# The first third of w_mod in four column transfers, applied in two parts, and 330 operations in a new order

## The chip, the cores and the metric

The kernel runs on one core of a Trainium2 chip. The metric is the device time of one execution in microseconds. Before the change it is 325.63 us, the median of 3 runs (325.49 to 326.61). The profile is of one further execution, whose span from the first to the last instruction is 324.3 us.

## The reference, cut to what matters

A transformer block with conditioning: six vectors of 640 numbers come from one product of `silu(c)` with `w_mod`, and shift, scale and gate an attention with a sliding window of 256 and a gated MLP.

```python
mod = (silu(c) @ w_mod).reshape(1, 6, 1, -1)          # c: 1 x 640, w_mod: 640 x 3840
sa, ca, ga, sb, cb, gb = mod[:, 0], ..., mod[:, 5]
h = layernorm(x) * (1 + ca) + sa                      # x: 2048 x 640
x = x + ga * attention(h @ wqkv, window 256, 32 heads of 20) @ wo
h = layernorm(x) * (1 + cb) + sb
x = x + gb * ((sigmoid(h @ w_gate) * (h @ w_up)) @ w_down)
```

The change concerns `sa` and `ca`, the first two of the six vectors: columns 0 to 1279 of `w_mod`, which is its first third.

## The kernel before

The 2048 rows of `x` are taken in eight chunks of 256 rows (two blocks of 128). A chunk goes through layernorm, modulation, q/k/v projection, scores, exponentials, masks, the product with V, output projection, second layernorm and MLP. Chunks overlap: the projections of later chunks are mixed into the attention and the MLP of earlier ones.

The program first writes down a list of 2121 operations (`Prog.op`, L91). Each gets a number from the list `PRIO` (L342), by its place in the list of operations. `schedule` (L152) sorts by that number; the number modulo 5 names the engine (0 TensorE, 1 ScalarE, 2 VectorE, 3 GpSimd, 4 SyncE). So `PRIO` fixes both the engine of an operation and its place in that engine's queue, and each queue is worked off strictly in that order. `schedule` also estimates times, but uses them only to choose which buffer of a pool a tile gets. `emit` (L250) adds the semaphore waits: an operation waits for all that it reads and for the last users of its buffer.

**The loads at the start.** SyncE issues block 0 of `x`, then the first third of `w_mod` in five transfers of 128 rows each (`load_bulk` at L624, target `wd`; 2560 contiguous bytes per row), then `wqkv` in pieces of 320 columns for q and k (`load_w3`, L615, called at L626; 640 bytes per row and piece) and one piece of 640 columns for v. Between these stand further blocks of `x`. ScalarE issues `c` and block 1 of `x`.

**The modulation vectors.** TensorE first transposes `c` (L634); ScalarE and VectorE make `silu(c)` and spread it to 64 equal columns (`silubc`). `fnA` (L750) then multiplies each 128x128 tile of the loaded third with `silubc`: fifty matmuls of 64 columns, in five operations by rows (`kt`), each waiting for one transfer, all accumulating in one tile of PSUM, `psA`. Between them stand short filler matmuls on zeros (`fill`, L657, instructions at L660). One VectorE copy (L761) takes the result to `mA`, which holds shift and scale for the five column tiles of 128 (`dt` 0 to 4).

**Chunk 0.** VectorE normalizes blocks 0 and 1 (L796), TensorE transposes them, two small matmuls per `dt` (`pe_transposes`, L816; the one of `dt` 4 goes to a free bank of `psA`), ScalarE and VectorE copy the five results to `hT` (L839) and then modulate `hT` in place, ten operations of 128x128, one per `dt` and block (L846, L847). All ten read `mA`. Then the projections begin: for a block and a piece of 320 columns there are five matmuls over `kt` in two operations (`pe_chain`, L674), the first with `kt` 0 and 1, the second with `kt` 2 to 4. They wait for their piece of `wqkv` and for their parts of `hT`.

**Before the first transposes** TensorE runs ten matmuls on zeros (`warm`, L646, instructions at L649).

Of the kernel before, what the change touches and what calls it, by code (L numbers as in the profile page):

```python
# [13 lines left out]
D = 640  # L14
# [3 lines left out]
NDT = D // 128  # L18
# [7 lines left out]
SWITCH = 0.095  # L26
ENGATTR = {"pe": "tensor", "act": "scalar", "dve": "vector", "pool": "gpsimd", "sp": "sync"}
ENGS = ("pe", "act", "dve", "pool", "sp")
OVERLAP = {"pe": 0.0, "act": 0.085, "dve": 0.075, "pool": 0.045, "sp": 0.0}
# [52 lines left out]
class Prog:  # L82
# [69 lines left out]
    def schedule(self):  # L152


        free = {e: START for e in ENGS}
        bw = 0.0
        lastturn = False
        order = {e: [] for e in ENGS}
        dmacnt = [0] * NDMA
        dmalast = [None] * NDMA  # L160
        rr = 0
        pemode = 0
        portend = 0.0
        freed = {}

        def slot_time(pool, s):
            ten = pool.tenant[s]
            if ten is None:
                if not all(x.done for x in pool.init[s]):
                    return None  # L170
                return max([x.end + x.lat for x in pool.init[s]], default=0.0)
            return None if ten.left else freed[ten]

        def take(t, s):
            ten = t.pool.tenant[s]
            t.prev = list(t.pool.init[s]) if ten is None else list(ten.rel)
            t.slot = s
            t.pool.tenant[s] = t

        for o in sorted(self.ops, key=lambda x: x.prio):  # L180
            assert all(d.done for d in o.deps), o.tag
            e = ENGS[o.prio % 5]
            assert e in o.engs, (o.tag, e)
            o.eng = e
            st = max([o.tmin, free[e] + (SWITCH if e == "pe" and o.mode != pemode else 0.0)]
                     + [d.end + (0.0 if d.eng == "pe" and e == "pe" else d.lat) for d in o.deps])
            if o.isdma and e == "sp":
                st = max(st, bw - QMAX)
            for t in o.tiles:
                if t.slot is None:  # L190
                    step = 1 if t.mate is None else 2
                    best = None
                    for s in range(0, len(t.pool.tenant), step):
                        rts = [slot_time(t.pool, s + k) for k in range(step)]
                        if None not in rts and (best is None or max(rts) < best[0]):
                            best = (max(rts), s)
                    assert best is not None, (o.tag, t.name)
                    if t.mate is None:
                        take(t, best[1])
                    else:  # L200
                        take(t, best[1] + t.odd)
                        take(t.mate, best[1] + 1 - t.odd)
                for x in t.prev:
                    st = max(st, x.end + x.lat)
            if e == "dve" and o.port:
                st = max(st, free["pool"])
            elif e == "pool":
                st = max(st, portend)
            o.start = st
            if e == "pe":  # L210
                pemode = o.mout
            dur = o.dur[e]
            free[e] = st + dur - OVERLAP[e]
            if e == "dve" and o.port:
                portend = free[e]
            if o.isdma:
                turn = o.dlat > 3.0
                if e == "sp" and bw - st > 2.0:
                    free[e] += 0.35 if o.dur[e] > 1.0 else 0.1
                bw = max(st + o.dlat, bw + (MIXED if turn != lastturn and bw > st + o.dlat else 0.0)) + o.work  # L220
                lastturn = turn
                o.end = max(bw - 0.83, st + dur)
                s = rr
                rr = (rr + 1) % NDMA
                dmacnt[s] += 16
                o.key, o.val = f"d{s}", dmacnt[s]
                if dmalast[s] is not None:
                    o.deps.append(dmalast[s])
                dmalast[s] = o
            else:  # L230
                o.end = st + dur
            order[e].append(o)
            o.done = True
            for t in o.tiles:
                t.left -= 1
                if t.left == 0:
                    last = {}
                    for x in t.ops:
                        if x.isdma:
                            last[x] = x  # L240
                    for e2 in ENGS:
                        xs = [x for x in t.ops if x.eng == e2 and not x.isdma]
                        if xs:
                            last[e2] = max(xs, key=lambda x: x.start)
                    t.rel = list(last.values())
                    freed[t] = max(x.end + x.lat for x in t.rel)
        self.order = order
        self.span = max(o.end for o in self.ops)
# [88 lines left out]
def c_pe(n):  # L337
# [3 lines left out]
PE_EPS = 0.14  # L341
PRIO = [  # L342
# [132 lines left out]
MW = 64  # L475
# [831 lines left out]
```

## Time and profile before

| | us |
|---|---|
| median of 3 runs | 325.63 |
| lowest, highest | 325.49, 326.61 |
| span of the profiled execution | 324.3 |
| busy in it: TensorE | 317.3 |
| busy: VectorE, ScalarE, GpSimd | 211.8, 212.3, 187.2 |
| moved by DMA | 37.85 MB, 117 GB/s on average |

From 4 us to 20 us the DMA engines are kept busy: the windows of 4 us there show between 352 and 378 GB/s. TensorE's busy time counts each matmul to a modelled end, so that pipelined matmuls overlap; a busy share near 100% means that the queue did not run dry, and the step from one matmul's start to the next says how fast it went.

The lines of the profile stand with the prediction. In a timeline a row is: start, duration, engine, line of the kernel, operation, target<-sources with their shapes, count of instructions merged into the row, and in brackets the idle time before it with what ended it. PE is TensorE's matmul, PEld its weight load, which may run ahead of the matmul; DVE is VectorE, ACT ScalarE, POOL GpSimd, SP SyncE. A row of windows gives for a stretch its length, then for each engine the busy time and the number of instructions, the granted clock, the busy share of the DMA engines, and GB/s.

### The profile page before, as it was taken

The numbers are of one execution on the slowest core, as the hardware profiler recorded it, in microseconds if no ns is written. First come the engines' busy times: TensorE is split into PE (matmuls) and PEld (weight loads), VectorE is DVE, ScalarE is ACT, GpSimd is POOL, SyncE is SP. The second block draws the span as 40 slices with busy tenths as digits, with TensorE's granted clock in tenths as the row PEclk, the third lists the DMA queues.
The fourth block names the chain that finished last, engine by engine and source line by source line (L and its number), as shares of the span: only waits on it lengthen the run. The fifth ranks groups of instructions, "written<-read, shape, count | busy, mean of one in ns | idle before, by whom it ended". The sixth has DMA issues, their size and how long they took to land.

```text
span 324.3 us, 11594 instructions
## 1 busy us (share of the span) xinstructions
PE 317.3 (98%) x4872; PEld 222.7 (69%) x4873; DVE 211.8 (65%) x424; ACT 212.3 (65%) x316; POOL 187.2 (58%) x276
## 2 busy tenths in 40 slices
PE   8999999989999999999999999999999999999997
PEld 3564545446776568765776467877786788787885
DVE  5797898778687959674477475837463769264332
ACT  1899985889876687788687867786767764011120
POOL 5128869976668694847585939382939691012100
DMA  7998799989891383824405394340213032202101
GB/s 249 371 333 299 165 269 180 200 137 183 260 164 22 83 109 77 152 61 101 85 22 82 97 103 110 92 69 5 81 40 88 3 79 53 76 20 64 40 2 40
DMA packets 71694, 37.85 MB, mean 117 GB/s; under 512 B 45274, under 2 KB 70362, under 8 KB 71642
## 3 DMA queue, kind: packets, MB, share of 16 engines
q1 hardware_dynamic: 69616, 35.31, 48.3%
q10 hardware_dynamic: 2026, 1.80, 2.1%
q8 instruction: 38, 0.62, 0.8%
q14 instruction: 14, 0.11, 0.1%
HBM read 21.30 MB, written 5.25 MB: 82 GB/s over the span
## 4 chain that ended last, share of the span: by engine, by line
PE 73%; DMA 2%; SPq 2%; DVE 1%; POOL 1%; issue 0%; DVEq 0%
PE M L668 61%; PE S L669 6%; PE M L669 5%; DMA gbc<-gate 2%; SPq L803 2%; DVE wd L1192 1%; POOL x L793 0%; POOL st L788 0%; DVE hh L1211 0%; POOL E L1040 0%; DVE x L1230 0%; DVEq L310 0%
## 5 line engine op out<-in xcount | busy, mean ns | idle before, releaser
L1040 POOL TENSOR_SCALAR_AFFINE_SELECT E<-E 128x512 bf16<-128x512 bf16 (+1 forms) x176 | 142.6, 836 | 68.7 <-ACT E L1015 67.0
L1015 ACT ACTIVATE E<-S 128x512 bf16<-128x512 f32 (+2 forms) x184 | 150.9, 878 | 47.4 <-PE S L669 46.5
L668 PE MATMUL M<-wqkv,hT 128*128 128x480 bf16 (+1 forms) x340 | 73.9, 355 | 0.6 <-ACT hT L846 0.5
L668 PE MATMUL M<-h2T,wu 128*128 128x256 bf16 x480 | 68.0, 273 | 0.5 <-DVE hh L1211 0.5
L668 PE MATMUL M<-h2T,wg 128*128 128x256 bf16 x480 | 67.8, 273 | 0.0
L668 PE MATMUL M<-wd,hh 128*128 128x320 bf16 (+2 forms) x396 | 58.1, 295 | 0.0
L1209 ACT ACTIVATE sig<-M 128x512 f32<-128x512 f32 x48 | 28.9, 602 | 44.1 <-PE M L668 41.7
L1211 DVE SCALAR_TENSOR_TENSOR hh<-sig,M 128x512 bf16<-128x512 f32 x48 | 32.4, 681 | 37.1 <-ACT sig L1209 24.0
L668 PEld LDWEIGHTS M<-h2T,wu 128*128 128x128 bf16 x480 | 45.9, 98 | 8.4 <-issue 1.2
L668 PEld LDWEIGHTS M<-h2T,wg 128*128 128x128 bf16 x480 | 45.7, 98 | 7.1
L668 PEld LDWEIGHTS M<-wqkv,hT 128*128 128x128 bf16 x340 | 30.1, 98 | 27.6 <-DMA wqkv<-in_A_wqkv_dram 1.6
L668 PEld LDWEIGHTS M<-wd,hh 128*128 128x128 bf16 x396 | 36.8, 98 | 14.3 <-DVE hh L1211 0.2
L669 PEld LDWEIGHTS S<-QT,KT 20*64 20x64 bf16 (+1 forms) x1856 | 19.9, 100 | 21.3 <-ACT E L1015 12.0
L1230 DVE TENSOR_TENSOR x<-M,x 128x320 bf16<-128x320 f32 (+2 forms) x33 | 15.6, 476 | 27.2 <-PE M L668 27.2
L669 PE MATMUL S<-QT,KT 20*64 20x256 bf16 (+5 forms) x1856 | 32.1, 228 | 1.2 <-ACT E L1015 1.2
L776 DVE BATCH_NORM_STATS2 st<-x 128x6 f32<-128x320 bf16 x64 | 28.6, 477 | 2.3 <-DMA x<-in_A_x_dram 1.9
L1082 DVE STREAM_TRANSPOSE T<-M 128x512 f32<-128x512 f32 x32 | 21.5, 698 | 9.2 <-PE S L669 8.0
L668 PE MATMUL M<-wo,oT 128*128 128x320 bf16 x160 | 25.4, 299 | 0.0
L669 PE MATMUL M<-E,V 128*32 128x128 bf16 (+1 forms) x960 | 22.8, 246 | 0.8 <-ACT E L1015 0.4
L781 POOL TENSOR_SCALAR st<-st 128x2 f32<-128x2 f32 x16 | 3.7, 234 | 33.8 <-DVE st L778 33.6
L669 PEld LDWEIGHTS M<-E,V 128*32 128x32 bf16 x960 | 19.2, 97 | 5.3 <-issue 2.9
L1091 DVE STREAM_TRANSPOSE On<-Tn 128x1024 bf16<-128x1024 bf16 x16 | 19.8, 1240 | 0.3
(77 smaller groups left out, 240.2 us busy)
## 6 DMA issues: line engine op xcount, KB each, us to landing
x<-in_A_x_dram SPq DMA_DIRECT2D x23, 160.0 KB, 2.3
doc<-On SPq DMA_DIRECT2D x56, 40.0 KB
wd<-in_B_w_down_dram SPq DMA_DIRECT2D x4, 480.0 KB
wd<-in_w_mod_dram SPq DMA_DIRECT2D x5, 320.0 KB
wqkv<-in_A_wqkv_dram SPq DMA_DIRECT2D x4, 400.0 KB
wu<-in_w_mod_dram SPq DMA_DIRECT2D x5, 320.0 KB
oT<-doc SPq DMA_DIRECT2D x8, 192.0 KB, 2.5
out_dram<-x SPq DMA_DIRECT2D x9, 160.0 KB
```

What stands on the lines that cost most here:

```text
L668: return e.matmul(o, l, r, start=st, stop=sp, skip_group_check=True)
L669: return e.matmul(o, l, r, start=st, stop=sp, tile_position=tp, skip_group_check=True)
L776: A("dve", lambda e, g, bi=bi, j=j: e.bn_stats(v(bi * 12 + j * 6, 6), src[bi].ap[:, j * 320:(j + 1) * 320]), 0.48, reads=[src[bi].r()], wr ...
L781: A("pool", lambda e, g: e.tensor_scalar(v(28, n), var(), EPS, None, op0=ALU.add), 0.2, reads=[st.r(("m", bi)) for bi in range(n)], writes ...
L803: return e.dma_start_transpose(dst(), src())
L1015: A("act", lambda e, eng: e.activation(dst(), src(), ACT.Exp, scale=SM_SCALE), c_act(n), reads=[Sp.r()], writes=[E.r(key)], prio=3, tag=f" ...
L1040: A("pool", lambda e, eng: e.affine_select(rows(dst), rows(src), pattern=[[0, 8], [sign, n]], compare_op=ALU.is_ge, fill=0.0, base=base, c ...
L1082: A("dve", lambda e, g, h=h: e.transpose(T1.ap[:, 512 * h:512 * h + 512], X[h].ap), 0.694, reads=[X[h].r()], writes=[T1.r(h)], prio=3.5, t ...
L1091: A("dve", lambda e, g: e.transpose(On.ap[:], Tn.ap[:]), 1.22, reads=[Tn.r()], writes=[On.r()], prio=4, tag=f"tr2_{a}")
L1209: A("act", lambda e, g, pg=pg, sg=sg: e.activation(sg.ap[:], pg.ap[:], ACT.Tanh, scale=0.5), c_act(512), reads=[pg.r()], writes=[sg.r()], ...
L1211: A("dve", lambda e, g, pu=pu, sg=sg, f0=f0: e.scalar_tensor_tensor(out=hh.ap[:, f0:f0 + 2, :], in0=sg.ap[:].rearrange("p (a b) -> p a b", ...
L1230: A("dve", lambda e, g, ps=ps, bi=bi, c0=c0, n=n: e.tensor_tensor(x1[bi].ap[:, c0:c0 + n], ps.ap[:, 0:n], x1[bi].ap[:, c0:c0 + n], op=ALU. ...
```

## The change

1. The first third of `w_mod` comes in four transfers by columns: scale tiles 0 to 2, shift tiles 0 to 2, scale tiles 3 and 4, shift tiles 3 and 4. The first two are 128 x 5 pieces of 768 bytes, the last two of 512 bytes.
2. `fnA` becomes four operations, one per transfer, each over all five `kt`. They accumulate in two banks of `psA`, and two VectorE copies take the result to `mA`: tiles 0 to 2 after the second transfer, tiles 3 and 4 after the fourth. A modulation of chunk 0 reads only its own part. The matmul that opens the accumulation becomes two.
3. Of the fillers, two single ones stay; a third single one and a double one after the last `fnA` go.
4. Block 4 of `x` is issued behind `wqkv`'s v piece instead of ahead of the second q piece.
5. `PRIO` is new. The second part of every engine's queue keeps its order (the last 816 of TensorE's operations, 279 of ScalarE's, 338 of VectorE's, 224 of GpSimd's, 179 of SyncE's); ahead of it the order differs.
6. `schedule` no longer estimates times; the buffer of each tile stands in a new list `SLOTS`, which holds the same buffers that the estimate gave before.

```diff
-    load_bulk(wm_ap[0], wm_src[:, :, 0:1280], Rm[0], 0.93, 0.2, "wm0", lat=0.9)
+    CG = (range(0, 3), range(3, 5))
+    PIECES = [(G, bank) for G in range(2) for bank in (1, 0)]
+    R_wc = {x: R(f"wc{x[0]}{x[1]}") for x in PIECES}
+    for k, (G, bank) in enumerate(PIECES):
+        lo, hi = bank * D + CG[G][0] * 128, bank * D + CG[G][-1] * 128 + 128
+        dma(lambda lo=lo, hi=hi: wm_ap[0][:, :, lo:hi], lambda lo=lo, hi=hi: wm_src[:, :, lo:hi], 0.0036 * (hi - lo),
+            writes=[R_wc[G, bank]], prio=0.2 + 0.01 * k, tag="wm0", lat=0.9)
...
-    for kt in range(NDT):
-        def fnA(e, g, kt=kt):
-            for bank in (1, 0):
-                for cg in range(5):
-                    ins = mm(e, psA.ap[:, bank, cg * MW:cg * MW + MW],
-                             wm_ap[0][:, kt, bank * D + cg * 128:bank * D + cg * 128 + 128], silubc[:, kt, 0:MW],
-                             kt == 0 and cg == 0 and bank == 0, kt == NDT - 1)
+    for n, (G, bank) in enumerate(PIECES):
+        def fnA(e, g, G=G, bank=bank):
+            for kt in range(NDT):
+                for cg in CG[G]:
+                    j = (1 - bank) * len(CG[G]) + cg - CG[G][0]
+                    ins = mm(e, psA.ap[:, G, j * MW:j * MW + MW],
+                             wm_ap[0][:, kt, bank * D + cg * 128:bank * D + cg * 128 + 128], silubc[:, kt, 0:MW], False, kt == NDT - 1)
             return ins
-        if 0 < kt < 4:
+        if 0 < n < 3:
             fills.append(fill(FILL, oA[-1:]))
...
-    fills.append(fill(2 * FILL, oA[-1:]))
-    A("dve", lambda e, g: e.tensor_copy(mA[:], psA.ap[:, 0:2, 0:5 * MW].rearrange("p b (a m) -> p b a m", m=MW)[:, :, :, 0]), 0.18,
-      reads=[psA.r()], writes=[R_mA], prio=0)
+        if bank == 0:
+            lo, hi = CG[G][0], CG[G][-1] + 1
+            A("dve", lambda e, g, G=G, lo=lo, hi=hi: e.tensor_copy(
+                mA[:, :, lo:hi], psA.ap[:, G, 0:2 * (hi - lo) * MW].rearrange("p (b a m) -> p b a m", b=2, m=MW)[:, ::-1, :, 0]), 0.18,
+              reads=[psA.r((G, 1)), psA.r((G, 0))], writes=[R_mAg[G]], prio=0, tag="mAc")
...
-                    A(("act", "dve"), mo, {"act": 0.44, "dve": 0.28}, port=True, reads=[dst.r(("t", dt))] + Rmod, writes=[dst.r((dt, bi))],
+                    A(("act", "dve"), mo, {"act": 0.44, "dve": 0.28}, port=True, reads=[dst.r(("t", dt)), Rmod[dt > 2]], writes=[dst.r((dt, bi))],
```

The two lists `PRIO`, read as queues, begin as follows (q0 is the projection of block 0 with the first q piece, k0 the one with the first k piece; a and b are a chain's first operation, `kt` 0 and 1, and its second, `kt` 2 to 4; T is a transposition on TensorE of projected q or k).

| queue | before | after |
|---|---|---|
| SyncE | x0, five of w_mod, q piece 1, k piece 1, x3, x2, k piece 2, x4, q piece 2, v piece, x5 | x0, four of w_mod, q piece 1, k piece 1, x3, x2, k piece 2, q piece 2, v piece, x4, x5 |
| TensorE | fnA, fill, fnA, fill, fnA, fill, fnA, transposes of `dt` 1, 0, 2, 3, 4, last fnA, double fill, q0a, q0b, k0a, k0b, block 1 q a and b, T, T, block 1 k a, ... scores | fnA scale 0-2, fill, fnA shift 0-2, fill, fnA scale 3-4, transposes of `dt` 1, 4, 0, 2, 3, fnA shift 3-4, q0a, k0a, k0b, q0b, block 1 q a and b, block 1 k a, T, T, ... scores |
| VectorE | normalize x1, x0, copy to hT twice, copy to `mA`, modulate 6 times, statistics of x3 and x2, ... statistics of x4 | normalize x1, x0, first copy to `mA`, copy to hT once, modulate `dt` 1 and 0 of block 0, second copy to `mA`, modulate 6 times, statistics of x2 and x3, ... |
| ScalarE | copy to hT three times, modulate 4 times, take out q0, k0 | copy to hT four times, modulate twice, take out k0, q0 |

Up to the first score matmuls TensorE has the same projections and transpositions in both lists.

More of the change, by code (lines that the diff above doesn't have):

```diff
@@ L152, in schedule @@
     def schedule(self):
-        free = {e: START for e in ENGS}
-        bw = 0.0
-        lastturn = False
         order = {e: [] for e in ENGS}
@@ L161, in schedule, with number @@
         rr = 0
[L162 to L178, printed above, removed]
+        tiles = {}
+        def number(t):
+            if t is not None and t not in tiles:
+                tiles[t] = len(tiles)
+                number(t.mate)
+        for o in self.ops:
+            for t in o.tiles:
+                number(t)
         for o in sorted(self.ops, key=lambda x: x.prio):
@@ L184, in schedule @@
             o.eng = e
[L185 to L188, printed above, removed]
             for t in o.tiles:
                 if t.slot is None:
[L191 to L215, printed above, removed]
-            if o.isdma:
[L217 to L223, printed above, removed]
-                rr = (rr + 1) % NDMA
[L225 to L231, printed above, removed]
+                    s = SLOTS[tiles[t]] if SLOTS else 0
@@ new lines, in schedule @@
+                    ten = t.pool.tenant[s]
+                    assert ten is not None or all(x.done for x in t.pool.init[s]), (o.tag, t.name)
+                    assert ten is None or ten.left == 0, (o.tag, t.name)
+                    t.prev = list(t.pool.init[s]) if ten is None else list(ten.rel)
+                    t.slot = s
+                    t.pool.tenant[s] = t
+            if o.isdma:
+                dmacnt[rr] += 16
+                o.key, o.val = f"d{rr}", dmacnt[rr]
+                if dmalast[rr] is not None:
+                    o.deps.append(dmalast[rr])
+                dmalast[rr] = o
+                rr = (rr + 1) % NDMA
@@ L237, in schedule @@
                     last = {}
[L238 to L244, printed above, removed]
+                    for x in sorted(t.ops, key=lambda x: x.prio):
+                        last[x if x.isdma else x.eng] = x
                     t.rel = list(last.values())
-                    freed[t] = max(x.end + x.lat for x in t.rel)
         self.order = order
-        self.span = max(o.end for o in self.ops)
     def emit(self):
@@ L338, in c_pe @@
     return max(n, 64) / 2400.0 + 0.0027
-PE_EPS = 0.14
 PRIO = [
[117 rows of a table removed]
[116 rows of a table added]
+]
+SLOTS = [
[20 rows of a table added]
 ]
@@ L466 @@
 DSAFE = 1.5
-START = 0.8
-PORTLAG = 0.05
-MIXED = 0.55
 NPB = 0
@@ L484 @@
 WSE = (("dve", "pool"), ("dve", "pool"))
-QMAX = 4.5
 WDT = 72.0
@@ L743, in build, with ones @@
     A("pool", lambda e, g: e.memset(Eall[:, 1, 0:5 * MW], 1.0), 0.3, writes=[R_one], prio=0)
-    p_E.init[1].append(A("pe", lambda e, g: mm(e, psA.ap[:, 1, 0:5 * MW], ident[:], Eall[:, 1, 0:5 * MW], True, False), 0.14,
-                         reads=[R_one, R_ident], writes=[psA.r()], prio=0, lat=0.2, tag="modA"))
+    def ones(e, g):
+        for G in range(2):
+            ins = mm(e, psA.ap[:, G, 0:len(CG[G]) * MW], ident[:], Eall[:, 1, 0:len(CG[G]) * MW], True, False)
+        return ins
@@ L746, in build @@
+    one_o = A("pe", ones, 0.14, reads=[R_one, R_ident], writes=[psA.r((G, 1)) for G in range(2)], prio=0, lat=0.2, tag="modA")
+    p_E.init[1].append(one_o)
     oA = []
     fills = []
-    for kt in range(NDT):
-        def fnA(e, g, kt=kt):
-            for bank in (1, 0):
-                for cg in range(5):
-                    ins = mm(e, psA.ap[:, bank, cg * MW:cg * MW + MW],
-                             wm_ap[0][:, kt, bank * D + cg * 128:bank * D + cg * 128 + 128], silubc[:, kt, 0:MW],
-                             kt == 0 and cg == 0 and bank == 0, kt == NDT - 1)
+    for n, (G, bank) in enumerate(PIECES):
[5 more added lines that the diff above has]
+                             wm_ap[0][:, kt, bank * D + cg * 128:bank * D + cg * 128 + 128], silubc[:, kt, 0:MW], False, kt == NDT - 1)
@@ L755, in fnA @@
             return ins
-        if 0 < kt < 4:
+        if 0 < n < 3:
             fills.append(fill(FILL, oA[-1:]))
-        oA.append(A("pe", fnA, 0.42, reads=[Rm[0][kt], R_silubc], writes=[psA.r()], prio=0, lat=0.2, tag="modA",
-                    extra=fills[-1:]))
-    fills.append(fill(2 * FILL, oA[-1:]))
-    A("dve", lambda e, g: e.tensor_copy(mA[:], psA.ap[:, 0:2, 0:5 * MW].rearrange("p b (a m) -> p b a m", m=MW)[:, :, :, 0]), 0.18,
-      reads=[psA.r()], writes=[R_mA], prio=0)
+        oA.append(A("pe", fnA, 0.042 * NDT * len(CG[G]), reads=[R_wc[G, bank], R_silubc], writes=[psA.r((G, bank))], prio=0, lat=0.2,
+                    tag="modA", extra=fills[-1:] + [one_o]))
@@ L883, in ln1 @@
         if a < NPH:
-            turned[a] = pe_transposes(src, t, scA, shA, [R_mA], 1, a)
+            turned[a] = pe_transposes(src, t, scA, shA, R_mAg, 1, a)
         else:
@@ L887, in ln1 @@
                                     [src[bi].r()], [t.r(("t", bi))], 1.26, f"atr{a}") for bi in range(2)]
-            modulate(t, scA, shA, [R_mA], 11, "a", a)
+            modulate(t, scA, shA, R_mAg, 11, "a", a)
     def evac(dst, src, n, reads, writes, prio, tag, extra=()):
```

4 lines of the change are left out of this document (1 added, 3 removed), and 253 rows, old and new, of tables (PRIO, SLOTS).

## The prediction

> **What bounds the kernel now.** I read the page first, then TensorE's busy time in four stretches, then its waits, and last the timeline of the start.
>
> ```profile
> span 324.3 us, 11594 instructions
> ...
> PE 317.3 (98%) x4872; PEld 222.7 (69%) x4873; DVE 211.8 (65%) x424; ACT 212.3 (65%) x316; POOL 187.2 (58%) x276
> ...
> PE 73%; DMA 2%; SPq 2%; DVE 1%; POOL 1%; issue 0%; DVEq 0%
> ```
> ```profile
> 0.00:10.36 10.36, 8.35 (x76) 4.14 (x78) 5.92 (x20) 2.98 (x7) 4.73 (x25) 1.00 0.82 272
> 10.36:36.00 25.64, 25.62 (x297) 15.39 (x301) 21.29 (x52) 23.27 (x44) 12.49 (x20) 1.00 0.91 301
> 36.00:86.50 50.50, 47.94 (x806) 27.52 (x798) 41.65 (x86) 41.78 (x63) 40.46 (x57) 1.00 1.01 206
> 86.50:324.30 237.80, 235.35 (x3698) 175.63 (x3698) 142.91 (x269) 144.22 (x205) 129.52 (x176) 1.00 0.35 71
> ```
> ```profile
> PE S L669 <- ACT E L1015: 1.2, 4, 0.4
> PE M L668 <- DVE hh L1211: 0.5, 1, 0.5
> PE M L669 <- ACT E L1015: 0.4, 1, 0.4
> PE M L669 <- DVE hT L858: 0.3, 1, 0.3
> ```
>
> The first number behind a stretch's length is TensorE's busy time. From its first projection at 10.36 us TensorE is busy 25.62 of 25.64 us, and in the last 237.8 us it waits for nothing that the profile names. Only between 36 and 86.5 us does it stand still, 2.4 us in seven waits (the third fence, window 36 to 90 us). So the kernel is a TensorE queue of fixed content behind a start of 10.36 us. A change at the start is worth what it moves that queue's beginning, and what the 2.4 us give or take.
>
> The start:
>
> ```profile
> 7.58 0.80 DVE L796 TENSOR_SCALAR x<-x,st 128x640 bf16<-128x640 bf16 x2 [1.22 <-POOL st L783]
> 8.10 0.17 PEld L668 LDWEIGHTS S<-silubc,wd 128*128 128x128 bf16 x4 [0.49 <-DMA wd<-in_w_mod_dram]
> 8.44 0.62 PE L668 MATMUL M<-ident,x 128*128 128x128 bf16 x8
> 8.76 0.76 DVE L839 CAST hT<-M 128x256 bf16<-128x256 f32 x2 [0.38 <-PE M L668]
> 8.88 0.66 ACT L839 ACTIVATE hT<-M 128x256 bf16<-128x256 f32 x2 [4.27 <-PE M L668]
> 9.01 0.45 PE L668 MATMUL S<-silubc,wd 128*128 128x64 bf16 x10
> 9.50 0.17 DVE L761 COPY mA<-S 128x10 f32<-128x10 f32 x1
> 9.71 0.31 DVE L847 TENSOR_SCALAR hT<-hT,mA 128x128 bf16<-128x128 bf16 x1
> 9.77 0.49 ACT L846 ACTIVATE hT<-hT,mA 128x128 bf16<-128x128 bf16 x1
> 10.36 2.33 PE L668 MATMUL M<-wqkv,hT 128*128 128x320 bf16 x15 [0.47 <-ACT hT L846]
> 11.16 1.20 PEld L668 LDWEIGHTS M<-wqkv,hT 128*128 128x128 bf16 x10 [0.21 <-DMA wqkv<-in_A_wqkv_dram]
> ```
>
> Three chains meet here. Blocks 0 and 1 are normalized by 8.38; the transposes follow at 8.44. The fifth transfer of w_mod lets the last fnA run at 9.01, `mA` is there at 9.67, and ScalarE's first modulation ends at 9.77 + 0.49 = 10.26: that releases the first projection, q0, at 10.36. The second, k0, starts at 11.16, when its piece of `wqkv` lands. q0 has five matmuls, so before the change the time until 11.16 is used for q0, and k0 starts on arrival.
>
> **The change part by part.**
>
> *Four column transfers.* They carry the same 5 x 320 KB = 1.64 MB, in 1280 packets of 768 bytes and 1280 of 512 instead of 640 of 2560. The nearest rows: a stretch filled with 2560-byte packets, and one filled with the 640-byte packets of `wqkv`; the last number is GB/s.
>
> ```profile
> 4.00:7.50 3.50, 3.50 (x38) 1.95 (x38) 1.93 (x7) 0.21 (x1) 1.41 (x4) 1.00 1.00 359
> 8.50:10.00 1.50, 1.34 (x24) 0.90 (x22) 1.20 (x5) 1.12 (x4) 0.00 (x0) 1.00 1.13 360
> 10.00:12.00 2.00, 1.64 (x12) 0.95 (x13) 1.55 (x7) 1.76 (x5) 0.00 (x0) 1.00 1.11 373
> ```
>
> 359 against 360: no difference, so I take 0 and let k0's piece land at 11.1 as before. Bounds: at the 373 of the third row 1.64 MB take 0.17 us less; and if a 512-byte packet cost as much as a 640-byte one (409,600 bytes in 640 packets, 1.14 us at 360 GB/s), 1280 of them would take 2.28 instead of 1.82 us, 0.46 more.
>
> The Trainium skill speaks against the smaller pieces (DMA: Bandwidth & Descriptors, "Why small descriptors are slow (HBM only)"): about three cycles of overhead for each packet, on beats of 32 bytes. By that rule 1280 x (27 + 19) beats stand against 640 x 83, 11% more, an estimate of 0.5 us on the 4.6 us of the transfers. The two rows at 359 and 360 do not show it: packets of a quarter the size moved as much. By the rule the sum below would be 0.5 us worse.
>
> *Applied in two parts.* By bytes, three fifths have landed where the third row transfer ended and four fifths where the fourth did (8.10). The first two fnA are done before that, so the first `mA` copy (0.17) lies in VectorE's idle time after 8.38 and costs nothing. The third fnA takes the fourth's place, about 0.3 us, so the transposes stay at 8.44. The first ScalarE copy to `hT` starts at about 8.76, as the first copy does now, and the first two, `dt` 1 and 0, take 0.66, to 9.42; VectorE modulates `dt` 0 0.31 later, at 9.75 with the handing over, without waiting for the last transfer. q0a could then run at 9.85 (before, 0.10 passed from 10.26 to 10.36), its `wqkv` piece lands at about 10.0 (one piece, 1.14 us, ahead of 11.12). So q0a starts at 10.0, 0.36 us earlier.
>
> *What follows it in the queue.* Behind q0a's two matmuls now stands k0a, and k0 is not there before 11.16. q0b, which could run, stands behind k0b. So TensorE waits from 10.3 to 11.16, and everything in its queue waits too: no modulation, however early, helps.
>
> ```profile
> 11.16 1.53 PE L668 MATMUL M<-wqkv,hT 128*128 128x320 bf16 x10
> 12.54 0.45 PEld L668 LDWEIGHTS M<-ident,stg 128*128 128x128 bf16 x8 [0.18 <-ACT stg L893]
> 14.76 0.52 PEld L668 LDWEIGHTS M<-wqkv,hT 128*128 128x128 bf16 x5 [0.31 <-DMA wqkv<-in_A_wqkv_dram]
> 15.55 0.40 PE L669 MATMUL S<-QT,KT 20*128 20x256 bf16 x8
> ```
>
> Ten matmuls take 12.54 - 11.16 = 1.38 us, 0.138 each. Before, five are left at 11.16 to finish q0 and k0; now eight: 3 x 0.138 = **+0.41 us**.
>
> *x4 behind v.* The second q piece no longer has 160 KB ahead of it, 0.164 MB / 360 GB/s = 0.46 us. Its wait at 14.76 (0.31 of the weight load, which runs one matmul ahead, so 0.31 - 0.14 = 0.17 of TensorE) goes: **-0.17 us**. x4's two statistics now come after its landing behind v, when VectorE is at 4.00 of 4.00; they are hidden by gaps behind it:
>
> ```profile
> 13.89 0.43 DVE L776 BATCH_NORM_STATS2 st<-x 128x6 f32<-128x320 bf16 x1
> 20.00:24.00 4.00, 4.00 (x49) 2.68 (x48) 4.00 (x10) 3.21 (x7) 1.83 (x2) 1.00 0.94 311
> 26.59 0.66 DVE L894 CAST stg<-M 128x480 bf16<-128x480 f32 x1 [0.54 <-PE M L668]
> 28.29 1.32 DVE L1082 STREAM_TRANSPOSE T<-M 128x512 f32<-128x512 f32 x2 [1.04 <-PE M L669]
> ```
>
> One statistic (0.43) was early; its move is covered by 0.54 + 1.04 of idle time. Without that cover it costs 0.43.
>
> *Fillers, the second opening matmul, the second copy.* They lie in TensorE's waits ahead of q0a or in VectorE's; nothing.
>
> *The rest of the order.* Up to the scores at 15.55 the same TensorE work stands in both lists; from about 36 us on the order is the old one. Between, both have the same work and TensorE is full, so I take 0; the bounds are -0.3 (the wait for hT at 38, in the third fence) and +0.4 (the same once more, behind VectorE's order there).
>
> Sum: 0.41 - 0.17 = 0.24 us on TensorE's queue, 324.3 to 324.5 in the span. The runs' median lies 1.3 us over this span; so 325.63 + 0.24, about **325.9 us**.
>
> **The rivals.**
>
> *The waits between 36 and 86.5 shrink.* The order ahead of them decides how far ScalarE and VectorE are when TensorE comes by. For it: they are waits for other engines, 2.4 us in all. Against: these engines get their input from TensorE, so a shift moves both. If half goes: -1.2 + 0.24, 324.7 us; all, 323.5.
>
> *The small packets cost time.* At 0.46 k0 starts at 11.62: 325.9 + 0.46 = 326.3 us. Against it stand the two equal rates.
>
> *VectorE loses its cover.* It is full from 20 to 24; with x4's 0.43 and one more wait for hT of 0.4 the sum is 326.7 us.
>
> *TensorE falls back to half speed: slower.* The same 512-column matmul is slow at the start and fast later:
>
> ```profile
> 1.31 2.74 PE L649 MATMUL S<-E 128*128 128x512 bf16 x6 [1.31 <-DVE E L644]
> 3.98 0.18 PE L634 MATMUL M<-ident,oT 5*128 5x5 bf16 x1
> 6.46 0.38 PE L660 MATMUL S<-E 128*128 128x512 bf16 x1
> 6.67 0.46 PE L668 MATMUL S<-silubc,wd 128*128 128x64 bf16 x10
> ```
>
> Six starts from 1.31 to 3.98 are about 0.43 us each; at 6.46 one takes 0.21. Some 5 us of work came before the change of speed (the clock column says 1.00 throughout and does not show it). Three fillers are gone, and TensorE now waits 0.85 us before k0. If that drops it back, 5 us of work take twice their time, 2.5 us lost: 328.4 us. It decides from the point where an idle stretch of 0.85 us is enough; one of 0.47 (at 10.36) was not.
>
> The Trainium skill (TensorE: Matmul & The Clock Gate, "What's actually happening") gives the window of this gate as about 3.4 us, so 0.85 us of waiting should not trip it; the matmuls at 0.138 after the wait at 10.36 agree as far as they go.
>
> **How the numbers follow.** The forecast has 0.48 (its own range 325.4 to 326.4, by -0.17 and +0.46), shorter waits 0.22, small packets 0.13, VectorE 0.11, half speed 0.06. I call 0.5%, 1.6 us, no change: 324.0 to 327.3 us. Faster than that needs nearly all of the 2.4 us: 0.13 of the 0.22. Slower takes half speed's 0.06 and, with further waits, 0.09 of the packets' and VectorE's cases: 0.15. That leaves 0.72. The range goes from 324.0, where the first rival is three quarters true, to 327.4, the VectorE case with the packets' 0.46 and some of the later waits.
>
> **What would show it.** Right: TensorE's first projection at about 10.0, two matmuls, a gap to 11.1 ended by the DMA of `wqkv`, no wait for `wqkv` at about 14.8, scores at 15.8, and waits from 36 on as before. Wrong: k0's piece landing after 11.5 or before 10.8; matmuls of 320 columns at 0.27 after the gap; the 2.4 us of waits by over 1 us larger or smaller. If TensorE has no gap before k0, the main term falls.

## The result and the profile after

| | before | after |
|---|---|---|
| median of 8 runs each, us | 325.56 | 326.85 |
| lowest, highest | 325.12, 326.61 | 326.40, 327.74 |
| ratio after / before, 95% interval | | 1.0037 (1.0024 to 1.0051) |
| span of the profiled execution | 324.3 | 326.0 |

By the ratio the kernel is 0.8 to 1.7 us slower, inside the 0.5% that the prediction called no change, but clearly not its +0.24. The profiled execution is the slowest of the eight after (327.74); the spans of the others are 324.7 to 325.7. So the time lies in the prediction's range (324.0 to 327.4) because that range is wide. At the start the pattern came as forecast (two matmuls, a gap that ends with the DMA of `wqkv`, no wait for the second q piece), but not the times, and the prediction's sign of being wrong, k's piece landing after 11.5 us, came true (11.95). Of the later runs two single executions, one of a_qfirst (676.43 us, granted clock 0.474) and one of b_cols (401.25 us, clock 1.00), count in the medians below but not in the ratios.

The page after:

```profile
span 326.0 us, 11592 instructions
...
PE 316.9 (97%) x4871; PEld 222.5 (68%) x4871; DVE 212.5 (65%) x428; ACT 211.0 (65%) x313; POOL 187.0 (57%) x276
...
PE 82%; DMA 7%; DVE 3%; SPq 3%; ACT 3%; issue 2%; ACTq 0%; DVEq 0%
```

DMA has 7% of the chain of work that ended last, against 2% before; but the chain of before adds up to 79% of its span only, so the two shares can't be compared. The same four stretches as before, the last one to the new end:

```profile
0.00:10.36 10.36, 7.80 (x75) 3.77 (x75) 5.67 (x19) 2.60 (x6) 5.34 (x30) 1.00 0.87 246
10.36:36.00 25.64, 24.44 (x280) 14.93 (x280) 22.06 (x54) 21.66 (x40) 10.77 (x16) 1.00 0.98 309
36.00:86.50 50.50, 48.66 (x823) 28.04 (x816) 40.85 (x87) 41.84 (x63) 40.70 (x55) 1.00 1.01 201
86.50:326.00 239.50, 236.04 (x3703) 175.77 (x3701) 143.94 (x271) 144.91 (x207) 130.19 (x177) 1.00 0.35 72
```

Between 10.36 and 36 us TensorE was busy 25.62 us and is now busy 24.44: 1.20 us of standing still, where before there was next to none. TensorE's timeline says where (the bracket is the idle time ahead of the row):

```profile
9.73 0.47 PE L639 MATMUL S<-silubc,wd 128*128 128x64 bf16 x10
10.86 0.45 PE L639 MATMUL M<-wqkv,hT 128*128 128x320 bf16 x2 [0.67 <-DMA wqkv<-in_A_wqkv_dram]
11.99 2.21 PE L639 MATMUL M<-wqkv,hT 128*128 128x320 bf16 x15 [0.69 <-DMA wqkv<-in_A_wqkv_dram]
...
16.63 0.40 PE L640 MATMUL S<-QT,KT 20*128 20x256 bf16 x8
```

q0a starts at 10.86 instead of 10.36 (0.50 later), and 0.69 us of waiting follow it: 1.19 together. k0 starts at 11.99 instead of 11.16 (+0.83), the scores at 16.63 instead of 15.55 (+1.08). Both waits end with a piece of `wqkv`. What happens behind the start is nearly as before; here are TensorE's waits between 36 and 90 us after (total, number, longest):

```profile
PE S L640 <- ACT E L992: 0.9, 3, 0.4
PE M L639 <- DVE hh L1188: 0.5, 1, 0.5
PE M L640 <- ACT E L992: 0.4, 1, 0.4
PE M L640 <- DVE shB L708: 0.3, 1, 0.3
```

2.1 us against 2.4. One more wait of 0.5 us stands at 94.45 (for the DMA of `oT`), in this execution alone.

Why the pieces of `wqkv` are late is in the windows of the start; the last number is GB/s. Before:

```profile
2.00:4.00 2.00, 2.00 (x6) 0.48 (x4) 0.89 (x2) 1.08 (x1) 2.00 (x10) 1.00 0.88 276
4.00:6.00 2.00, 2.00 (x7) 0.81 (x7) 1.60 (x6) 0.21 (x1) 0.45 (x1) 1.00 1.01 355
6.00:8.00 2.00, 1.92 (x34) 1.25 (x32) 0.75 (x4) 0.00 (x0) 1.01 (x3) 1.00 0.98 352
8.00:10.00 2.00, 1.74 (x31) 1.30 (x32) 1.58 (x7) 1.12 (x4) 0.00 (x0) 1.00 1.11 354
```

After:

```profile
2.00:4.00 2.00, 2.00 (x6) 0.53 (x5) 0.84 (x3) 1.08 (x1) 2.00 (x10) 1.00 0.77 203
4.00:6.00 2.00, 2.00 (x8) 0.75 (x7) 1.54 (x7) 0.21 (x1) 0.61 (x4) 1.00 1.09 364
6.00:8.00 2.00, 1.28 (x33) 0.97 (x32) 0.80 (x3) 0.00 (x0) 1.29 (x4) 1.00 1.17 307
8.00:10.00 2.00, 1.63 (x35) 1.16 (x31) 1.39 (x6) 0.74 (x3) 0.16 (x3) 1.00 1.16 320
```

In bytes, the changed kernel falls behind by 2 us x (73 - 9 + 45 + 34) GB/s = 286 KB, at 360 GB/s 0.79 us: k's piece landed at 11.12 before and at 11.95 after. From 6 to 8 us most packets are of 512 bytes, and there the DMA engines are busier (share 1.17 against 0.98) and move less. The other part, some 0.36 us, is lost between 2 and 4 us, ahead of the 512-byte packets.

### The profile page after: what moved, and what is told of

It is laid out like the page before. It is cut to its first block, busy times and chain, and to the rows that moved or that the text cites. A ratio compares the mean times of both kernels' runs of the same rounds, so it can differ in the third digit from the quotient of the medians.

```text
span 326.0 us, 11592 instructions
## 1 busy us (share of the span) xinstructions
PE 316.9 (97%) x4871; PEld 222.5 (68%) x4871; DVE 212.5 (65%) x428; ACT 211.0 (65%) x313; POOL 187.0 (57%) x276
## 4 chain that ended last, share of the span: by engine, by line
PE 82%; DMA 7%; DVE 3%; SPq 3%; ACT 3%; issue 2%; ACTq 0%; DVEq 0%
PE M L639 68%; PE S L640 7%; PE M L640 6%; SPq L535 3%; ACT E L992 2%; DMA wqkv<-in_A_wqkv_dram 2%; DMA gbc<-gate 2%; DMA doc<-On 2%; DMA oT<-doc 1%; DVE st L753 1%; DMA gate<-gq 1%; ACT hT L788 0%; ACTq L535 0%; DVE On L1068 0%; DVE Tn L1066 0%
## 5 line engine op out<-in xcount | busy, mean ns | idle before, releaser
L871 DVE CAST stg<-M 128x480 bf16<-128x480 f32 (+1 forms) x28 | 16.5, 600 | 7.6 <-PE M L639 7.5
```

Source lines behind the costliest of these rows:

```text
L871: return e.tensor_copy(dst(), src())
```

## The experiments

The theory they test: k0's start is set by the landing of k's piece, so by the bytes ahead of it and the rate at which they move; from k0 on TensorE is a queue of fixed content that passes its delay through to the end. The rivals: the new order, x4's place, the application in two parts. The main readings of the runs, from their traces (landing of k's piece by its last of 16 semaphore updates, start of k0 and of the first scores, us) with the ratio of the times. The later runs were made on three chips; the ratio of each is against the kernel before, run beside it on the same chip:

```
run          k lands  k0     scores  k0 to scores  median  ratio, 95% interval
before       11.12    11.16  15.55   4.39
b_1280       11.02    11.11  15.46   4.35          325.87  1.0001 (0.9989 to 1.0014)
b_512        11.79    11.83  16.22   4.39          326.17  1.0014 (1.0002 to 1.0026)
c_256        13.90    13.95  18.29   4.34          328.04  1.0062 (1.0044 to 1.0081)
b_x4         11.94    11.98  16.22   4.24          325.82  1.0003 (0.9994 to 1.0012)
c_order      11.72    11.76  16.40   4.64          326.00  1.0002 (0.9983 to 1.0021)
b_cols       12.21    12.25  16.65   4.40          326.26  1.0020 (1.0009 to 1.0031)
after        11.95    11.99  16.63   4.64          326.85  1.0037 (1.0024 to 1.0051)
after_again  12.09    12.14  16.78   4.64          326.69  1.0026 (1.0016 to 1.0037)
a_qfirst     12.02    12.06  16.30   4.24          326.51  1.0021 (1.0009 to 1.0033)
```

### The changed kernel again, beside its variants

No edit.

> The changed kernel once more, for comparison on the same chip. All theories: 1.0 to 1.3 us over the kernel before, k0 (the first projection that needs the first k piece of wqkv) at 12.0 us.

It is 1.0026 times the kernel before, and its times lie within 0.45 us, where the first eight lay within 1.34. The wait for `oT` is not there; k0 starts at 12.14 and the scores at 16.78, as in the first profile give or take 0.15 us. The ratio means 0.5 to 1.2 us more than before, where 1.0 to 1.3 were expected.

### q0b ahead of k0 again

```diff
 PRIO = [...]
+PRIO = [p // 5 * 500 + p % 5 for p in PRIO]
+for i, p in ((98, 38500), (107, 39000), (108, 41500), (99, 40001), (109, 42501),):
+    PRIO[i] = p
```

The numbers are spread out, then q0b goes ahead of k0a and k0b, and q0's eviction ahead of k0's; all else is the changed kernel's.

> The changed kernel with q0's second operation moved ahead of k0, as before the change. Theory 1 (TensorE's queue starts late, by the landing of the k piece plus what stands behind it): k0 still at 12.0 us, but five matmuls are left at that time instead of eight, so 0.41 us less than the changed kernel, 0.7 to 0.9 us over before. Theory 2 (the order at the start is of no account, the time is lost in later waits): as the changed kernel, within 0.2 us.

```profile
12.06 1.83 PE L642 MATMUL M<-wqkv,hT 128*128 128x320 bf16 x12 [0.27 <-DMA wqkv<-in_A_wqkv_dram]
...
16.30 0.29 PE L643 MATMUL S<-QT,KT 20*128 20x256 bf16 x4
```

In TensorE's timeline k0 waits for the same late piece (12.06), but the scores follow 4.24 us later instead of 4.64. The three matmuls are worth 0.40 us, about what three steps of 0.138 make. In the times the gain is 0.18 us between the medians, too small for the intervals.

### The order alone, in the kernel before

Transfers, application and x4 as before; k0a and k0b ahead of q0b, k0's eviction ahead of q0's.

```diff
...
+for i, p in ((110, 40000), (111, 40005), (101, 40010), (112, 40501), (102, 40506),):
+    PRIO[i] = p
...
```

> The kernel before with its transfers, its application in one part and its place of x4, but with k0a and k0b ahead of q0b on TensorE and k0's eviction ahead of q0's on ScalarE. Theory 'order': TensorE runs q0a's two matmuls at 10.4, stands until k's piece lands at 11.1, then has eight matmuls instead of five until both are done, so the scores start 0.41 us later than the 15.46 and 15.55 of the two profiles of this transfer pattern, at 15.9, and the time is 0.3 to 0.5 us over that of the kernel before. Rival 'the other end of the chain decides' (eviction and transposition of k0 come earlier by this order, and q0 has slack): scores at 15.5 as before, time within 0.2 us of the kernel before.

```profile
10.88 0.43 PE L644 MATMUL M<-wqkv,hT 128*128 128x320 bf16 x2 [0.47 <-ACT hT L822]
11.76 1.61 PEld L644 LDWEIGHTS M<-wqkv,hT 128*128 128x128 bf16 x13 [0.79 <-DMA wqkv<-in_A_wqkv_dram]
11.76 1.94 PE L644 MATMUL M<-wqkv,hT 128*128 128x320 bf16 x13 [0.46 <-DMA wqkv<-in_A_wqkv_dram]
```

As in b_x4 below, the buffers stand in a list that holds the ones of before, part 6 of the change. From k0 to the scores it takes 4.64 us, exactly as in the changed kernel, against 4.39: the order alone is worth +0.25 us, with x4 where it was. The scores at 16.40 are later than expected because in this execution k's piece landed at 11.72. The time cannot tell +0.25 from 0 (interval -0.6 to +0.7 us).

### x4 behind v alone, in the kernel before

```diff
...
+for i, p in ((27, 33504), (32, 34004), (235, 58004), (238, 80007),):
+    PRIO[i] = p
...
```

Block 4 goes behind the v piece and the second q piece takes its place; the first statistic of block 4 goes behind those of block 5.

> Part 4 alone: the kernel before with block 4 of x behind the v piece, and the first of its statistics after block 5's; buffers as before. Theory 1: the wait for the second q piece at 14.8 us goes, 0.17 us less, if VectorE's later gaps take the statistic; 0 to 0.4 us more if they don't.

From k0 to the scores it takes 4.24 us instead of 4.39: the wait for the second q piece is gone, 0.15 us. The time shows nothing (1.0003), and here too k's piece landed late in the profiled execution (11.94).

### The columns alone: the changed program with the order of before

The four column transfers, four `fnA`, two copies and fewer fillers of the changed kernel; `PRIO` is the old list, with the new operations in the places of the old ones.

> Part 1 to 3 of the change alone: column transfers, four fnA, two copies to mA, fewer fillers, with the order of before in all queues and block 4 of x where it was. Theory 1: k0 at 12.0 us as in the changed kernel, with q0 done by then: 0.8 us over before. Theory 2: below 0.3 us.

k's piece lands at 12.21 and the scores follow it by 4.40, as before. So with these transfers k0 starts 0.8 to 1.1 us later than in the profile of before, whatever the order, and the time is 1.0020 of before's. The application in two parts was not run without the columns; but k0's wait ends with the landing of its piece, not with a modulation.

One profile of before is a thin base: with row transfers the last update of k's piece came between 11.02 and 11.94 us. The first of its 16 updates, which a single late engine cannot hold back, separates the kernels better: 10.07 to 10.29 in the four with rows in packets of 2560 or 1280 bytes, 10.41 to 10.58 in the four with two column transfers of 1280-byte packets (below), 11.01 to 11.32 in the four with the changed kernel's transfers, 11.17 in b_512. So both the columns and the small packets cost time, the packets by these numbers the more.

### The packets alone: row transfers cut small

The kernel before with the rows' 2560 bytes written in pieces with a gap behind each, so that each piece is a packet (here 512 bytes; the other two have 1280 and 256).

```diff
-    load_bulk(wm_ap[0], wm_src[:, :, 0:1280], Rm[0], 0.93, 0.2, "wm0", lat=0.9)
+    wm0 = wd[:].rearrange("p a b -> p (a b)")[:, 0:7600].rearrange("p (t n c) -> p t n c", t=NDT, n=5)
+    for k in range(NDT):
+        dma(lambda k=k: wm0[:, k, :, 0:256], lambda k=k: wm_src[:, k, 0:1280].rearrange("p (n c) -> p n c", c=256), 0.93,
+            writes=[Rm[0][k]], prio=0.2 + 0.01 * k, tag="wm0", lat=0.9)
...
```

> The kernel before, with its five row transfers of the third cut into packets of 512 bytes (the target has a gap after every 256 columns); nothing else. In the changed kernel packets of 512 bytes ran at about 290 GB/s. Theory 1: 1.64 MB take 5.65 instead of 4.56 us, so k0 starts at 12.2 to 12.5 instead of 11.16 us, and the time grows by the same 1.0 to 1.4 us. Rival (packet size of no account): k0 within 0.2 us, time within 0.3 us. Theory 2 (the start is hidden by later waits): k0 late, time within 0.5 us.

> The same with packets of 1280 bytes. Theory 1: they run as fast as those of 2560; k0 at 11.1 to 11.3 us, time within 0.2 us of before. Rival (every split of a row costs): k0 0.3 us or more later.

> The kernel before with its five row transfers cut into packets of 256 bytes instead of 2560 (the target rows are spaced out; nothing else moves). In the two runs so far 512-byte packets moved at 306 to 308 GB/s in the stretch 6 to 8 us, where 640-byte packets moved at 360 and more. Theory 'a floor': a packet of up to about 512 bytes takes one and the same time on its engine, so 1.64 MB in 256-byte packets move at half of 307, 154 GB/s, 10.6 us instead of 4.6: q's and k's pieces land 6 us later than in the kernel before, the scores start at about 21.5 us instead of 15.55, and the time is about 331.5 us. Rival 'an overhead': a fixed overhead of about three beats of 32 bytes for each packet on top of its bytes, 11 beats for 8 of data against 83 for 80: 1.64 MB take about 6.1 us, k's piece lands 1.5 us later than in the kernel before, and the time is about 327.2 us. In both, what the piece of k loses reaches the scores one to one; if the end loses clearly less than the scores, the waits between 36 and 90 us take it up.

The windows with 512-byte packets, then those with 256-byte packets:

```profile
4.00:6.00 2.00, 2.00 (x7) 0.81 (x7) 1.71 (x7) 0.21 (x1) 0.44 (x1) 1.00 1.11 329
6.00:8.00 2.00, 2.00 (x34) 1.47 (x32) 0.75 (x4) 0.00 (x0) 1.00 (x3) 1.00 1.19 308
```
```profile
4.00:6.00 2.00, 1.60 (x7) 0.58 (x6) 1.69 (x7) 0.21 (x1) 0.44 (x1) 1.00 1.14 250
6.00:8.00 2.00, 1.13 (x22) 0.75 (x22) 0.76 (x4) 0.00 (x0) 1.00 (x3) 1.00 0.95 208
8.00:10.00 2.00, 0.91 (x13) 0.38 (x11) 0.37 (x2) 0.00 (x0) 0.00 (x0) 1.00 1.08 237
```

1280-byte packets cost nothing. 512-byte packets move at 308 GB/s and take k's piece 0.7 us later, 256-byte packets at 208 to 250 and 2.8 us later. b_512 came out smaller than its first theory: k0 at 11.83 instead of 12.2 to 12.5, and 0.45 us instead of 1.0 to 1.4 between the medians. Both theories of c_256 miss: a floor would have brought 6 us, the overhead of three beats 1.5. A packet does cost more than its bytes: at 237 GB/s one of 16 engines needs 256 x 16 / 237 = 17.3 ns for 256 bytes, at 308 GB/s 26.6 ns for 512, so about 8 ns come with each packet, an estimate by the straight line through these two (with 250 or 208 GB/s it is 6 or 13 ns). The line does not hold further up: for 640 bytes it gives 31 ns, and at the 360 GB/s of the prediction's row they take 28. This is the rule of the Trainium skill that the prediction weighed and set aside (DMA: Bandwidth & Descriptors, "Why small descriptors are slow (HBM only)"); the runs agree with its sign, and with 256 bytes they show nearly twice its loss. Why 256 bytes cost so much more is open; the DMA engines' busy share fell to 0.95 there from 6 to 8 us, so part may be gaps between packets.

The delay goes through one to one. First scores and first down-projection of three runs whose starts lie 2.8 us apart (b_1280, after_again, c_256):

```profile
15.46 0.40 PE L672 MATMUL S<-QT,KT 20*128 20x256 bf16 x8
...
96.69 0.30 PE L671 MATMUL M<-wd,hh 128*128 128x320 bf16 x1
```
```profile
16.78 0.40 PE L640 MATMUL S<-QT,KT 20*128 20x256 bf16 x8
...
97.99 0.43 PE L639 MATMUL M<-wd,hh 128*128 128x320 bf16 x2
```
```profile
18.29 0.29 PE L672 MATMUL S<-QT,KT 20*128 20x256 bf16 x4
...
99.55 0.43 PE L671 MATMUL M<-wd,hh 128*128 128x320 bf16 x2
```

From the scores to the down-projection these take 81.23, 81.21 and 81.26 us: the waits on the way give nothing back. Six more of the fourteen profiles lie between 81.2 and 81.35 and three between 81.4 and 81.7. Only the profiles of before and after need 81.98 and 82.56, with a wait of 0.5 for `hh` at 86.5 and 87.5 and that of 0.51 for `oT` in after; so the two spans differ by more than the start explains, and the later runs, without these waits, are the better pair. The end follows too: from the scores to the end of the span it is 308.0 to 308.1 us in eight profiles, whose scores start between 15.46 and 18.29, 308.2 to 308.5 in four, and 308.8 and 309.4 in those of before and after. So the late start is not hidden by later waits, as b_512's theory 2 had it.

### Two column transfers with 1280-byte packets: a miss

```diff
-    PIECES = [(G, bank) for G in range(2) for bank in (1, 0)]
+    PIECES = [(G, bank) for bank in (1, 0) for G in range(2)]
...
-    for k, (G, bank) in enumerate(PIECES):
-        lo, hi = bank * D + CG[G][0] * 128, bank * D + CG[G][-1] * 128 + 128
+    for k, bank in enumerate((1, 0)):
+        lo, hi = bank * D, bank * D + D
...
-            writes=[R_wc[G, bank]], prio=0.2 + 0.01 * k, tag="wm0", lat=0.9)
+            writes=[R_wc[0, bank], R_wc[1, bank]], prio=0.2 + 0.01 * k, tag="wm0", lat=0.9)
```

The second one has q0b ahead of k0 as well.

> The changed kernel with the third of w_mod in two column transfers of 1280-byte packets (scale, shift) instead of four of 768 and 512 bytes; order otherwise as changed, but for the two fnA on shift, which come after the transposes. Theory 1, with the size of the packets as the cause of the late landing: k0 at 11.1 to 11.3 us instead of 12.0, and 0.2 to 0.4 us over before is left, from the order. Rival (not the size of the packets but that the transfers go by columns, with 640 or more packets each): k0 at 11.7 or later, 0.8 us or more over before.

> Both of these edits in the changed kernel. Theory 1: what is left is block 4 of x behind v and the rest of the order; between 0.2 us less and 0.1 us more than before. Theory 2: still 0.8 us or more over before.

Both missed: 326.79 (1.0038, 1.0017 to 1.0060) and 327.07 (1.0039, 1.0020 to 1.0058). The packets did nearly what they should, k's piece lands at 11.50 and 11.05 where k0 was expected at 11.1 to 11.3. But in the profiled execution of the first, TensorE's timeline and the windows (the third number from the end is the granted clock) show something else:

```profile
7.97 0.38 PE L629 MATMUL S<-E 128*128 128x512 bf16 x1
9.88 0.40 PE L637 MATMUL M<-ident,x 128*128 128x128 bf16 x2 [1.53 <-DVE x L771]
...
12.87 3.36 PE L637 MATMUL M<-wqkv,hT 128*128 128x320 bf16 x12 [0.41 <-issue]
```
```profile
8.00:10.00 2.00, 0.47 (x8) 0.17 (x5) 0.99 (x2) 0.00 (x0) 1.22 (x4) 0.84 1.13 359
10.00:12.00 2.00, 2.00 (x30) 2.00 (x30) 0.46 (x2) 1.42 (x4) 0.00 (x0) 0.50 1.11 365
12.00:14.00 2.00, 1.59 (x14) 0.98 (x12) 1.85 (x10) 0.88 (x2) 0.00 (x0) 0.50 1.12 367
14.00:16.00 2.00, 2.00 (x9) 1.07 (x8) 1.97 (x7) 0.71 (x2) 0.00 (x0) 0.50 1.07 361
```

TensorE stands still for 1.53 us until the normalized block of `x`, and its clock falls to half for nearly 7 us. In the trace the granted clock is on record from 5.95 us, falls at 9.36 and comes back at 16.19: steps of 3.41 and 6.83 us, the second twice the first. The stretch of 3.41 us ahead of the fall, and the least busy one of that length that the changed kernel's own record gives:

```profile
5.95:9.36 3.41, 1.55 (x28) 0.91 (x27) 1.63 (x4) 0.00 (x0) 1.45 (x5) 1.00 1.09 369
```
```profile
9.15:12.56 3.41, 1.99 (x27) 1.22 (x25) 2.46 (x10) 2.09 (x6) 0.00 (x0) 1.00 1.12 360
```

With 1.55 us of work in it the clock fell, with 1.99 it held. The mean clock of a_wide's profiled execution is 0.99; 4 of the 12 executions here and 3 of the 8 of the second kernel have 0.99 or 0.995. In a_wide the two with 0.99 took 329.3 us, the eight with 1.00 between 325.8 and 326.9.

Fillers take the idle time away, in both kernels:

```diff
-            fills.append(fill(FILL, oA[-1:]))
+            fills.append(fill(FILL if n < 2 else 5 * FILL, oA[-1:]))
```

> The changed kernel with two column transfers of 1280-byte rows (a_wide), and with five filler matmuls instead of one behind the second filler's place, so that TensorE does not stand still from 8.0 us until the transposes. In a_wide 4 of 12 executions had a granted clock of 0.99 or 0.995, and the profiled one shows 0.50 from about 9 to 16 us behind 1.5 us of waiting. Theory 'idle drops the clock': with the fillers no execution shows less than 0.998, the spread of the times falls to about 1 us, and the median is 325.9 to 326.2 us: k's piece lands at 11.1 to 11.5, and what is left over the kernel before is the order's 0.4. Rival 'not the idle time': some executions keep a clock of 0.99 to 0.995 and the median stays at 326.6 or above.

> c_wide_fill with q0b ahead of k0 as in the kernel before. Theory (packets and order are the two losses, and a_wide_q hid that behind dropped clocks, which it had in 4 of 8 executions): no dropped clocks, scores at about 16.2 as in a_wide_q's profile at full clock, because there the second half's modulation and not the piece of wqkv sets q0 (10.97), and a time of 326.1 to 326.3 us, 0.1 to 0.2 under c_wide_fill at most. Rival: with the clock held the time reaches the kernel before's, within 0.2 us of it; then the application in two parts costs nothing.

The clock is held, 1.00 in all 24 executions. The times are not won: 326.71 (1.0022, 1.0003 to 1.0041) and 326.69 (1.0022, 1.0004 to 1.0041), spread from 325.9 to 327.8, where 325.9 to 326.3 were expected. In VectorE's and TensorE's timelines of the first one it can be seen why, beside VectorE's row of a_wide_q below:

```profile
6.59 0.89 DVE L751 BATCH_NORM_STATS2 st<-x 128x6 f32<-128x320 bf16 x2 [1.47 <-DMA x<-in_A_x_dram]
...
9.93 0.28 PE L637 MATMUL M<-ident,x 128*128 128x128 bf16 x2 [0.92 <-DVE x L771]
...
12.05 0.43 PE L637 MATMUL M<-wqkv,hT 128*128 128x320 bf16 x2 [0.66 <-issue]
```
```profile
5.51 0.89 DVE L751 BATCH_NORM_STATS2 st<-x 128x6 f32<-128x320 bf16 x2 [0.40 <-DMA x<-in_A_x_dram]
```

Block 1 of `x`, which comes beside the wide transfers, landed at 6.57 us instead of 5.49, and statistics, normalization, transposes and q0 (12.05 against 10.97) follow it by the same 1.1 us. It is late in three of the four profiled executions of wide transfers (6.51 to 6.57) and in none of those of row transfers (4.79 to 5.21). That the late block makes the upper part of the spread fits, but single times have no trace. No run beat the kernel before.

## Why the prediction was right or wrong

- **Bound: right.** A TensorE queue of fixed content behind its start: 81.2 us from the scores to the first down-projection, and 308.0 to 308.1 to the end, in runs whose start differs by 2.8 us. The rival in which the waits between 36 and 86.5 us shrink falls with it.
- **Four column transfers, "no difference, so I take 0": wrong, the step that failed.** It measured +0.83 us at k0 (11.16 to 11.99), and +1.00 at the first update of its piece (10.29 to 11.29). The two equal rates, 359 and 360, came from 2560- and 640-byte packets; the price of a packet does not show there, but one size further down it does: b_512 with 512-byte packets alone took k0 0.67 us later, with the whole third in such packets. By the windows the changed kernel's own 512-byte packets, two fifths of the bytes, cost 2 us x (45 + 34) GB/s = 158 KB, 0.44 us, an estimate, as the windows hold packets of 768 and 640 bytes too; that is the upper bound that the prediction had worked out and not taken (0.46). The rest, about 0.4, is the slower beginning, 203 GB/s from 2 to 4 us; the seven other profiles with column transfers, the wide ones among them, show 180 to 215 there, the six with row transfers 239 to 276, with packets of 256 as of 2560 bytes. So it goes with the columns, not with the packets' size; why was not tried.
- **Applied in two parts: 0.36 us earlier at q0a was counted on; it came 0.50 later.** The transfers of `w_mod` are late themselves, so all that was laid out lies half a microsecond late: the transposes start at 8.94 instead of 8.44, and VectorE's first two modulations, all that q0a needs, end at 9.71 + 0.55 = 10.26 instead of 9.75, no earlier than ScalarE's before. And q's piece landed at 10.82 instead of 10.0.

```profile
8.94 0.28 PE L639 MATMUL M<-ident,x 128*128 128x128 bf16 x2
...
9.71 0.55 DVE L824 TENSOR_SCALAR hT<-hT,mA 128x128 bf16<-128x128 bf16 x2
```

- **Order and x4, +0.41 - 0.17 = +0.24: right in the sum.** From k0 to the scores the changed kernel takes 4.64 us against 4.39, +0.25. The two are not separate, though: a_qfirst shows 0.40 for the order with x4 behind v, b_x4 -0.15 for x4 alone, but c_order has the whole +0.25 without moving x4. With k0 first the second q piece is needed 0.4 us later, and x4 ahead of it no longer makes it late. Taken first, x4 is worth -0.15 and the order then 0.40; with the order first, that has the whole 0.25 and moving x4 adds nothing.
- **The rest of the order, fillers, VectorE's cover: right at 0.** The 1.20 us that TensorE lost between 10.36 and 36 us are the 0.50 and 0.69 us of the start. The wait for `hT` behind 38 us is gone and one of 0.3 for `shB` has come.
- **Small packets as a rival: this is what happened**, 0.46 as its price and the slower beginning on top. With +0.83 in place of 0 the prediction's own sum is +1.07; the scores came 1.08 later, and the times show +1.2.
- **Half speed: did not happen** in the changed kernel, whose waits were 0.67 and 0.69 us. But it is near: a_wide fell to half speed behind 1.53 us, and its filled version with 0.92 did not. The prediction asked which single wait is enough; by the windows above it may as well be the work in 3.41 us, 1.55 against 1.99, and these runs do not tell the two apart. Its price, 2.5 us, is that of a slow stretch of 5 us, not of 5 us of work, which would lose 5; a_wide's two executions with 0.99 took 2.4 to 3.5 us more than those with 1.00. The Trainium skill (TensorE: Matmul & The Clock Gate, "What's actually happening") has an idle window of about 3.4 us before the clock falls; the trace agrees with the length (3.41), but the window was not idle, TensorE was busy for 1.55 us of it.
- **A bound of the prediction's working:** its own range's lower end, 325.4, does not follow from -0.17, which gives 325.7; it needs the -0.3 of the wait for `hT` too.

What stays open: the times say less than the traces (b_512 +0.45 in the median where k0 was 0.67 later, c_256 +2.20 where it was 2.79); the cause of the slower beginning is not known; and +0.25 for the order is shown by the traces only.

## What to carry to other kernels

Where a queue of fixed content waits for its first operand, count the bytes ahead of that operand and the rate of their packets; an earlier helper result is worth nothing there, and here the smaller transfers made even that late. Equal rates at two packet sizes say nothing of a third that is smaller: take the bound, not the zero. And look at what the first transfers run beside: with fewer, larger transfers another load on the path came 1.1 us later in three of four profiles, and no gain was left.

## What the runs showed of the hardware that was not expected

Two kernels with the row transfers of before, unchanged up to there, had k's piece 0.6 to 0.8 us late in their profiled executions. The first of its 16 updates came as in the kernel before, the last did not:

```
run      k's piece: first and last of 16 updates   longest packet of w_mod behind 4 us
before   10.29  11.12                              0.91 us
b_x4     10.21  11.94                              1.47 us, at 6.29
c_order  10.07  11.72                              1.19 us, at 4.30
```

The median 2560-byte packet took 0.10 us between 6 and 8 us in the kernel before. The update before the last came at 11.12 in b_x4 and 10.76 in c_order, so one of the sixteen engines fell behind, and the whole transfer with it. That one long packet did it fits b_x4; which engine a packet was on is not in the trace, and c_order has several long ones. In the profiled executions in which w_mod came in packets of 768 bytes or less, none of these took over 0.5 us from 4 us on. This may be why small packets cost less in the median time than in the traces; it was not tried.
